# Attention output transposed by DMA from the second stage on, in a planned kernel of sparse attention and a gated FFN

## The chip, the cores and the metric

The kernel runs on one core of a Trainium2 chip. The metric is device time in microseconds, the median of several executions. Engines are named as in the profile: PE (TensorE; PEld is its weight load), DVE (VectorE), ACT (ScalarE), POOL (GpSimd), SP (SyncE, which issues the DMAs of the kernel before).

## What is computed

Attention over 4 batches, 8 heads, 768 positions and 64 dims, in which each query sees only the six chunks of 32 keys with the highest upper bounds; then a gated FFN over the 3072 tokens (512 to 1536 to 512).

```python
ub = sum(maximum(q * k_min, q * k_max), axis=-1)      # per chunk of 32 keys, causal chunks only
top_chunks = argsort(ub)[..., -6:]
scores = where(sel & causal, scale * q @ k.T, -1e9)
attn = softmax(scores)
x = (attn @ v) as [3072, 512]
out = (sigmoid(x @ w_gate) * (x @ w_val)) @ w_out
```

## The kernel before

**Stages.** The work is cut into eight stages s: batch s // 2, half s % 2 of its 384 query rows. A stage has four parts. *Load*: k, q and v come from HBM by SP's DMAs (L330 to L353). *Prep* (L379 to L539): q is transposed on PE (qT, L428) and copied by ACT or DVE into Qcat (L439 to L443); DVE forms the minimum and maximum of k by chunk (tree, L406); PE multiplies them (the bound products ub, L504), DVE takes the six best, and PE transposes the selection (apT, L533); k is cast and transposed (kT, L485). *Attention* (L550 to L625): for each head, PE writes scores into a PSUM tile (sc, L574; in odd stages two tiles per head), ACT takes the exponential (L578), POOL masks the diagonal (L584), and PE multiplies with V (pv, L596). Every two heads DVE divides by the row sums (the norm, L606 and L608) and writes the result to `xnat`, [128 rows, 3 blocks, 512] in fp16. *FFN* (L628 to L679): for each of 12 blocks PE forms gate and value products from `xT`, the transposed attention output (L646), ACT a tanh (gate, L652), DVE their product (hglu, L654); then PE forms three output tiles (o, L663), which ACT or DVE copies (osb, L670, L672) and SP stores (L678).

**The transposed attention output.** The FFN needs `xT`, two tiles per stage of [128, 2, 384]. After every four heads (L612 to L625), six PE transposes of 128x128 go into one PSUM tile of pool `m` (xtp, L621), and DVE or ACT copies it into `xT` (L624).

**The weights.** w_gate, w_val and w_out are loaded in twelve pieces of 768 KB (L367, L369) and cast by POOL or ACT (L373).

**What sets the order.** Nothing is scheduled at run time. Each step is a task with a due time, a duration per engine on which it can run, what it reads and writes, and its tiles (`Plan.add`, L70). `Plan.order` (L92) plays the tasks through: an engine takes, of those that can start within 0.12 us of the first, the one with the earliest due time. A tile of a pool can be taken only when the tile that used its buffer has been released. The result is one fixed order of instructions on each engine, with semaphore waits between them. Due times are offset by the table `NUDGE` (L22), by kind of task and by part and stage. PSUM pools are `big` (2 buffers), `m` (3) and `p` (1).

**Zero products.** When PE would idle in the planned time, the plan puts in products of zeros (`fill`, L266, and L153 to L157) that write a PSUM tile of their own in pool `p`, as long as no task has taken a tile of `p`. The first task of `p` is a kT of stage 1.

Of the kernel before, what the change touches and what calls it, by code (L numbers as in the profile page):

```python
# [9 lines left out]
F16 = mybir.dt.float16  # L10
# [4 lines left out]
GUARD = 88.0  # L15


LATENCY = {"PE": 0.22, "ACT": 0.08, "DVE": 0.06, "POOL": 0.12, "SP": 3.0}

NUDGE = {  # L22
    "v": -63.6, "Ap": -59.1, "kch": -0.4, "qch": 1.0, "wst": 2.5, "w": -706.6, "vn": -2.4, "k160": -402.8,
    "prep:0": -235.2, "tr0": 174.3, "qT0": -58.5, "Qc0": 634.5, "hq0": 22.2, "kmm0": -340.1, "kmT0": -375.7,
    "kc0": -22.3, "kT0": -50.7, "hk0": 28.9, "ub0": -139.5, "ubs0": -377.3, "ubq0": 660.7, "mx80": -334.1,
    "Ap0": -606.7, "apT0": -328.7, "mq0": -24.9, "sc0": 448.0, "attn:0": -226.6, "at0": -197.0, "pv0": 158.8,
    "xn0": 67.3, "xtp0": -203.0, "xT0": 61.1, "gv0": 102.6, "ffn:0": -24.2, "gate0": 2.6, "hglu0": -419.8,
    "o0": 643.0, "osb0": 108.2, "out0": 110.6, "k16": 506.3, "prep:1": -123.8, "tr": 10.9, "qT": -3.8, "Qc": 9.8,
    "hq": 30.7, "kmm": 15.3, "kmT": -75.4, "kc": -333.7, "kT": 3.0, "hk": 405.3, "ub": -252.3, "ubs": 344.4,
    "ubq": 8.6, "mx8": -27.8, "apT": -21.5, "mq": -5.9, "sc": -2.4, "attn:1": -132.3, "at": -49.8, "pv": -8.1,  # L30
    "xn": -608.2, "xtp": -111.2, "xT": -347.1, "gv": -3.0, "ffn:1": -26.5, "gate": -349.5, "hglu": -801.6, "o": 13.1,
    "osb": 197.5, "out": 206.7, "load:2": -53.5, "prep:2": -24.9, "attn:2": -15.6, "ffn:2": -5.1, "load:3": -28.9,
    "prep:3": -36.5, "attn:3": -33.1, "ffn:3": 8.2, "load:4": 32.8, "prep:4": -46.9, "attn:4": 31.7, "ffn:4": 18.4,
    "load:5": 20.2, "prep:5": 0.5, "attn:5": -135.7, "ffn:5": 19.7, "load:6": 25.4, "prep:6": 17.0, "attn:6": 15.6,
    "ffn:6": 217.4, "load:7": -0.8, "prep:7": 63.5, "attn:7": -95.3, "ffn:7": 359.4,
}
PARTS = {"load": ("kch", "qch", "vn", "v"), "attn": ("sc", "at", "pv", "xn", "xtp", "xT"),
         "ffn": ("gv", "gate", "hglu", "o", "osb", "out")}


# [9 lines left out]
class Plan:  # L50
# [8 lines left out]
    def __init__(self, slots, banks, cold_until=0.0, filler=None):  # L59
        self.slots = slots  # L60
        self.filler = filler
        self.banks = banks
        self.tasks = []
        self.writers, self.readers = {}, {}
        self.tile_tasks = {}
        self.cold_until = cold_until
        self.stage = None
        self.kinds = []

    def add(self, prio, options, r=(), w=(), tiles=(), port=False):  # L70
        i = len(self.tasks)

        key = w[0] if w else "-"
        kind = "const" if isinstance(key, str) else key[1] if key[0] in self.banks or key[1] == "gv" else key[0]
        names = nudged(kind, self.stage)
        self.kinds.append(names)
        prio += sum(NUDGE.get(x, 0.0) for x in names)
        deps = set()
        for key in r:
            deps.update(self.writers.get(key, ()))  # L80
            self.readers.setdefault(key, []).append(i)
        for key in w:
            deps.update(self.writers.get(key, ()))
            deps.update(self.readers.get(key, ()))
            self.writers[key] = [i]
            self.readers[key] = []
        deps.discard(i)
        for t in tiles:
            self.tile_tasks.setdefault(t, []).append(i)
        self.tasks.append((prio, options, deps, tuple(tiles), port))  # L90

    def order(self):  # L92
        n = len(self.tasks)
# [6 lines left out]
        free = {}  # L100
# [23 lines left out]
        while cand:  # L124
# [25 lines left out]
            us = self.tasks[i][1][o][1]  # L150
            if eng == "PE" and t < self.cold_until:
                us *= 2
            if eng == "PE" and self.filler and not rings[self.filler[0]]:  # L153
                each = self.filler[1] * (2 if t < self.cold_until else 1)
                fills = int((t - max(free.get("PE", 0.0), 1.0) - 0.15) / each)
                if fills > 0:
                    out.append((t - fills * each - 0.1, len(out), None, fills))  # L157
            end[i], eng_of[i] = t + us, eng
            free[eng] = t + us
            if eng == "POOL" or (eng == "DVE" and self.tasks[i][4]):  # L160
# [23 lines left out]
def kernel(  # L184
# [22 lines left out]
    R2 = CH // 2  # L207
    NST = 2 * B
    FC = D_FF // 4

    SB = {"ld": 3, "wld": 2, "vld": 2, "k16": 1, "tree": 1, "Qcat": 1, "headQ": 2, "kmx": 2, "kmm": 2, "ubs": 2,
          "mx8": 2, "rz": 2, "at": 6, "xT": 6, "xnat": 2, "gate": 3, "osb": 3, "hglu": 18}
# [17 lines left out]
    wv16 = consts.tile([128, 4, D_FF], F16, tag="wv16")  # L230
    wo16 = consts.tile([128, NFB, 512], F16, tag="wo16")

    plan = Plan({**SB, **PS}, PS, cold_until=7.0, filler=("p", 0.22, None))
    add = plan.add

    def dve_or_act(fn, dve, act):
# [26 lines left out]
        h0 = max(h0, 1) if i == 0 else h0  # L263
        copy(hks[half][i][64:89, h0:h1, :], first.to_broadcast([25, h1 - h0, HS]))

    def fill(n):  # L266

        ps = tl(("p", "fill"), [128, 512])
        for _ in range(n):
            nc.tensor.matmul(ps, zeros[:, 0:128], zeros, start=True, stop=True)  # L270

    def const_tasks():
        def _warm():
# [105 lines left out]
    def prep_tasks(s, t0, t1):  # L379
# [40 lines left out]
        for j in range(R2 // QR):  # L420
            qT = ("big", "qT", s, j) if alone else ("p", "qT", s, j)
            x = 0.05 + 0.1 * j

            def _t(j=j, qT=qT):
                ps = tl(qT, [128, QR, 128])
                for r in range(QR):
                    rr = QR * j + r
                    nc.tensor.transpose(ps[:, r, 0:RC], tl(("ld", "q", s))[0:RC, 128 * rr:128 * rr + 128], ident32[0:RC, 0:RC])  # L428
            add(at(x), [("PE", 0.40, _t)], r=[("qch", s, j), "id32"], w=[("qT", s, j)], tiles=[qT, ("ld", "q", s)])
            rs = slice(QR * j, QR * j + QR)  # L430
            for e in range(2):
                def src(j=j, e=e, qT=qT):
                    return tl(qT)[64 * e:64 * e + 64, :, 0:RC].rearrange("p r (c h) -> p h c r", h=H)

                def _raw(eng, sg, e=e, rs=rs, src=src):
                    dq = tl(("Qcat", s), [128, H, HS]).rearrange("p h (c r e) -> p h c r e", r=R2, e=2)
                    dst = dq[64 * sg:64 * sg + 64, :, :, rs, e]
                    if eng == "ACT":
                        nc.scalar.activation(dst, src(), AF.Relu if sg else AF.Copy)  # L439
                    elif sg:  # L440
                        nc.vector.tensor_scalar(dst, src(), 0.0, None, ALU.max)  # L441
                    else:
                        nc.vector.tensor_copy(dst, src())  # L443

                for sg in range(2):
                    add(at(x + 0.02), [("ACT", 0.49, lambda sg=sg, f=_raw: f("ACT", sg)),
                                       ("DVE", 0.56, lambda sg=sg, f=_raw: f("DVE", sg))][:1 if alone and j < 2 else 2],
                        r=[("qT", s, j)], w=[("Qc", s, j, e, sg)], tiles=[qT, ("Qcat", s)])
# [48 lines left out]
        for u in range(2):  # L497
# [5 lines left out]
                    h = 4 * u + i  # L503
                    nc.tensor.matmul(ps[32 * i:32 * i + 32, :], kcat[:, h, :], tl(("Qcat", s))[:, h, :], start=True, stop=True)  # L504
            x = 0.45 + 0.1 * u
            add(at(x), [("PE", 0.80, _ub)], r=qc_keys + [kkey], w=[ub], tiles=[ub, ("Qcat", s)])
            add(at(x + 0.02), [("DVE", 0.55, lambda ub=ub, ubs=ubs: nc.vector.tensor_tensor(
                tl(ubs, [128, HS]), tl(ub), penT[:, half, :], ALU.add))], r=[ub, "pen", 1, 2, 3], w=[ubs], tiles=[ub, ubs])

            def _ubq(ubs=ubs, ubq=ubq):  # L510
                ps = tl(ubq, [128, HB, 4, 32])
                for qb in range(HB):
                    nc.tensor.transpose(ps[:, qb].rearrange("p h c -> p (h c)"), tl(ubs)[:, 128 * qb:128 * qb + 128], ident32)
            add(at(x + 0.04), [("PE", 0.36, _ubq)], r=[ubs, "id32"], w=[ubq], tiles=[ubs, ubq])

            def _mx(ubq=ubq, mx8=mx8):
                m8, ps = tl(mx8, [128, HB, 4, 8]), tl(ubq)
# [32 lines left out]
    def attn_tasks(s, t0, t1):  # L550
# [12 lines left out]
        for h in range(H):  # L563
            x = h / (H + 0.5)
            for t, segs in enumerate(TILES[half]):
# [3 lines left out]
                def _sc(h=h, segs=segs, sc=sc):  # L569
# [4 lines left out]
                        nc.tensor.matmul(ps[:, 128 * o:128 * (o + n)], hk[:, h, jl:jl + 128],  # L574
                                         tl(("headQ", s))[:, h, 128 * (ib - q0):128 * (ib - q0 + n)], start=True, stop=True)
                add(at(x + 0.03 * t), [("PE", w / 2400 + 0.012 * len(segs), _sc)],
                    r=[hq_keys[h], ("mq", s, h)] + hk_keys + hkc, w=[sc], tiles=[sc, ("headQ", s)])
                add(at(x + 0.03 * t + 0.01), [("ACT", 0.19 + w * 0.815e-3, lambda sc=sc, a=a, w=w: nc.scalar.activation(  # L578
                    tl(a, [128, 1024], F16)[:, 0:w], tl(sc)[:, 0:w], AF.Exp, scale=scale))],
                    r=[sc], w=[a], tiles=[sc, a])  # L580
# [10 lines left out]
            for ib in range(q0, q0 + HB):  # L591
                def _pv(h=h, ib=ib, pv=pv):
# [3 lines left out]
                        nc.tensor.matmul(pvp[:, ib - q0, h % 2, :], tl(("at", s, h, t))[:, 128 * o:128 * o + 128],  # L596
                                         head_v(b, jb // HB)[:, h, jb % HB, :], start=(jb == 0), stop=(jb == ib))
                add(at(x + 0.9 / H + 0.01 * (ib - q0)), [("PE", 0.035 * (ib + 1), _pv)], r=ats + v_keys,
                    w=[("pv", s, h, ib)], tiles=[pv] + ats)
            if h % 2 == 1:  # L600
                hp = h // 2
                xn, rz = ("xnat", s), ("rz", s, hp)
# [1 line left out]
                def _norm(hp=hp, pv=pv, xn=xn, rz=rz):  # L604
# [4 lines left out]
                add(at(x + 0.95 / H + 0.03), [("DVE", 0.78, _norm)],  # L609
                    r=[("pv", s, hh, ib) for hh in (h - 1, h) for ib in range(q0, q0 + HB)], w=[("xn", s, hp)],  # L610
                    tiles=[pv, xn, rz])
            if h % 4 == 3:  # L612
                u = h // 4
                xtp, xT = ("m", "xtp", s, u), ("xT", s, u)

# [12 lines left out]
    def ffn_tasks(s, t0, t1):  # L628
# [4 lines left out]
        for fb in range(NFB):  # L633
# [7 lines left out]
            for i in range(2):  # L641
# [6 lines left out]
                for c0 in (0, 2):  # L648
                    add(at(x + 0.025 * i + 0.005 * c0), [("PE", 0.34, lambda c0=c0, f=_mm: f(c0))],
                        r=[("xT", s, 0), ("xT", s, 1), ("w", 2 * (fb // 3) + i)], w=[(s, "gv", i, fb)],  # L650
                        tiles=[gv[i], ("xT", s, c0 // 2)])
            add(at(x) - EV, [("ACT", 0.49, lambda gate=gate, ps=ps: nc.scalar.activation(  # L652
                tl(gate, [128, HS], F16), ps(0), AF.Tanh, scale=0.5))], r=[(s, "gv", 0, fb)], w=[gate], tiles=[gv[0], gate])
            add(at(x) - EV, [("DVE", 0.55, lambda gate=gate, hg=hg, ps=ps: nc.vector.scalar_tensor_tensor(  # L654
# [47 lines left out]
        ffn_tasks(s, T[s + 1] - (12 if s == 0 else 0) + 4, T[s + 1] + W + 4)  # L702
    with tc.manual_schedule():
        for i, o in plan.order():
            if i is None:
                fill(o)
            else:
                plan.tasks[i][1][o][2]()


# [28 lines left out]
```

## Time and profile before

| what | us |
|---|---|
| median of 3 runs (lowest, highest) | 340.85 (338.41, 341.76) |
| profiled execution, its own time | 340.61 |
| its span, first to last instruction | 338.9 |
| PE busy | 319.9 |
| DVE busy | 242.0 |
| ACT busy | 223.0 |
| POOL busy | 107.0 |

Busy times are unions: matmuls overlap, so the sum of durations is larger than the busy time, and what one instruction takes from PE is read from the distance of starts. A group's line gives line, engine, operation, output<-inputs, sizes and count, then busy us, mean ns of one, then the idle time of the engine just before and what ended it. In a timeline the columns are start, duration, engine, line, operation and count. "Granted clock" is the share of full speed that TensorE was given.

### The profile page before, as it was taken

To read this page: it belongs to the slowest core of one execution; us is meant where nothing else is said; L and a number is where in the kernel's file an instruction comes from. 1 tells how busy PE (TensorE), PEld (TensorE's weight loads), DVE (VectorE), ACT (ScalarE), POOL (GpSimd) and SP (SyncE) were. 2 spreads that over 40 slices of the span, in tenths; PEclk is the share of its full clock that TensorE was granted. 3 is DMA by queue.
4 is the path that set the end of the run, shared out by engine and by line. 5 is a ranking of instruction groups with operands and counts; after the bars stand their busy time and mean duration, and the time that the engine had idled before them with its cause. 6 is when DMAs were issued, how large, how long until landed. Compare 5 with 4: busy or idle time off the path is not lost.

```text
span 338.9 us, 7406 instructions
## 1 busy us (share of the span) xinstructions
PE 319.9 (94%) x2855; PEld 193.5 (57%) x2855; DVE 242.0 (71%) x642; ACT 223.0 (66%) x336; POOL 107.0 (32%) x147
## 2 busy tenths in 40 slices
PE   8886889979999989999999999999999999999995
PEld 3445445756457536675556556766666546775552
DVE  5779678869999899997986699886656257532430
ACT  5798964968467635886567669985856235993331
POOL 8278574553423330225110612240310030210000
PEclk9999699999999999999999999999999999999999
DMA  5997999977983150304630313000000010001002
GB/s 147 238 296 219 249 258 312 265 172 143 215 194 95 32 154 4 95 0 116 155 94 14 93 64 119 10 0 3 33 31 33 31 65 2 2 2 72 23 0 93
DMA packets 37947, 35.08 MB, mean 103 GB/s; under 512 B 25944, under 2 KB 30040, under 8 KB 36952
## 3 DMA queue, kind: packets, MB, share of 16 engines
q1 hardware_dynamic: 37912, 34.61, 37.6%
q8 instruction: 22, 0.36, 0.5%
q14 instruction: 13, 0.11, 0.1%
HBM read 28.31 MB, written 6.29 MB: 102 GB/s over the span
## 4 chain that ended last, share of the span: by engine, by line
PE 67%; DVE 14%; ACT 6%; POOL 5%; DMA 4%; issue 3%; DVEq 0%; ACTq 0%
PE m_o L663 15%; PE m_g L646 12%; PE m_v L646 11%; PE big_sc L574 7%; PE m_pv L596 5%; PE big_gv L646 5%; DMA wld<-in_moe_w_out_dram 4%; ACT Qcat L439 3%; PE p_qT L428 3%; DVE tree L406 3%; PE p_ub L504 3%; PE p_fill L270 3%; DVE hglu L654 2%; DVE Qcat L441 2%; DVE Qcat L443 2%
## 5 line engine op out<-in xcount | busy, mean ns | idle before, releaser
L578 ACT ACTIVATE at<-big_sc 128x896 f16<-128x896 f32 (+1 forms) x96 | 83.9, 916 | 12.3 <-PE big_sc L574 9.9
L646 PE MATMUL m_v<-xT,wv 128*128 128x384 f16 x336 | 72.7, 330 | 0.9 <-DVE hglu L654 0.9
L646 PE MATMUL m_g<-xT,wg 128*128 128x384 f16 x336 | 73.0, 330 | 0.5 <-DVE hglu L654 0.3
L663 PE MATMUL m_o<-wo,hglu 128*128 128x512 f16 x288 | 72.0, 379 | 0.0
L584 POOL TENSOR_SCALAR_AFFINE_SELECT at<-at 128x384 f16<-128x384 f16 x64 | 35.8, 562 | 108.2 <-ACT at L578 100.4
L652 ACT ACTIVATE gate<-m_g 128x384 f16<-128x384 f32 x84 | 41.0, 490 | 32.9 <-PE m_g L646 27.4
L654 DVE SCALAR_TENSOR_TENSOR hglu<-gate,m_v 128x384 f16<-128x384 f16 x84 | 46.0, 550 | 14.3 <-PE m_v L646 9.2
L646 PEld LDWEIGHTS <-wg 128*128 128x128 f16 x384 | 36.4, 99 | 24.9 <-issue 4.9
L646 PEld LDWEIGHTS <-wv 128*128 128x128 f16 x384 | 36.4, 99 | 24.6 <-issue 4.7
L574 PE MATMUL big_sc<-headQ,headK 89*128 89x128 f16 (+2 forms) x480 | 48.5, 240 | 0.7 <-DVE headQ L537 0.2
L663 PEld LDWEIGHTS <-hglu 128*128 128x128 f16 x288 | 26.2, 98 | 23.7 <-issue 1.9
L574 PEld LDWEIGHTS <-headK 89*128 89x128 f16 x480 | 32.2, 97 | 9.8 <-issue 2.0
L596 PEld LDWEIGHTS <-at 128*128 128x128 f16 x672 | 27.3, 98 | 15.3 <-ACT at L578 6.1
L455 POOL CAST headQ<-Qcat 64x768 f16<-64x768 f32 x31 | 26.1, 873 | 30.6 <-DVE Qcat L443 28.8
L596 PE MATMUL m_pv<-v,at 128*128 128x65 f16 x672 | 31.8, 194 | 3.8 <-POOL at L584 3.7
L670 ACT ACTIVATE osb<-m_o 128x512 f32<-128x512 f32 x20 | 11.9, 597 | 31.9 <-PE m_o L663 31.7
L406 DVE TENSOR_TENSOR tree<-tree 96x512 f32<-96x512 f32 (+2 forms) x48 | 28.9, 603 | 1.1
L393 POOL CAST k<-ld_k 96x1024 f16<-96x1024 f32 x12 | 14.1, 1190 | 47.8 <-PE p_kT L485 37.8
L443 DVE COPY Qcat<-p_qT 64x384 f32<-64x384 f32 x35 | 19.4, 555 | 13.5 <-PE p_qT L428 12.0
L439 ACT ACTIVATE Qcat<-p_qT 64x384 f32<-64x384 f32 x45 | 22.2, 493 | 6.8 <-PE p_qT L428 2.9
L406 DVE TENSOR_TENSOR tree<-ld_k 96x1024 f32<-96x1024 f32 (+1 forms) x18 | 20.6, 1149 | 2.1 <-DMA ld_k<-in_k_dram 2.0
L441 DVE TENSOR_SCALAR Qcat<-p_qT 64x384 f32<-64x384 f32 x32 | 17.8, 557 | 1.8 <-ACT Qcat L439 1.2
(91 smaller groups left out, 364.1 us busy)
## 6 DMA issues: line engine op xcount, KB each, us to landing
vld<-in_v_dram SPq DMA_DIRECT2D x24, 256.0 KB
out_dram<-osb SPq DMA_DIRECT2D x24, 256.0 KB
ld_k<-in_k_dram SPq DMA_DIRECT2D x5, 768.0 KB
ld_q<-in_q_dram SPq DMA_DIRECT2D x5, 768.0 KB
wld<-in_moe_w_gate_dram SPq DMA_DIRECT2D x4, 768.0 KB
wld<-in_moe_w_val_dram SPq DMA_DIRECT2D x4, 768.0 KB
wld<-in_moe_w_out_dram SPq DMA_DIRECT2D x4, 768.0 KB
ld_k<-in_k_dram SPq DMA_DIRECT2D x12, 192.0 KB
```

The lines of the kernel that those rows point to most:

```text
L406: nc.vector.tensor_tensor(dst[:, a:e], src[0:RC, a:e], src[0:RC, n + a:n + e], op)
L439: nc.scalar.activation(dst, src(), AF.Relu if sg else AF.Copy)
L443: nc.vector.tensor_copy(dst, src())
L455: eng.tensor_copy(tl(("headQ", s), [89, H, HS], F16)[0:64, h:h + 2, :], tl(("Qcat", s))[0:64, h:h + 2, :])
L574: nc.tensor.matmul(ps[:, 128 * o:128 * (o + n)], hk[:, h, jl:jl + 128], tl(("headQ", s))[:, h, 128 * (ib - q0):128 * (ib - q0 + n)], start ...
L578: add(at(x + 0.03 * t + 0.01), [("ACT", 0.19 + w * 0.815e-3, lambda sc=sc, a=a, w=w: nc.scalar.activation(tl(a, [128, 1024], F16)[:, 0:w], ...
L584: nc.gpsimd.affine_select(out=dg, in_=dg, compare_op=ALU.is_ge, fill=0.0, base=0, pattern=[[0, HB], [1, 128]], channel_multiplier=-1)
L596: nc.tensor.matmul(pvp[:, ib - q0, h % 2, :], tl(("at", s, h, t))[:, 128 * o:128 * o + 128], head_v(b, jb // HB)[:, h, jb % HB, :], start= ...
L646: nc.tensor.matmul(ps(i), w16[:, c, 128 * fb:128 * fb + 128], tl(("xT", s, c // 2))[:, c % 2, :], start=(c == 0), stop=(c == 3))
L652: add(at(x) - EV, [("ACT", 0.49, lambda gate=gate, ps=ps: nc.scalar.activation(tl(gate, [128, HS], F16), ps(0), AF.Tanh, scale=0.5))], r=[ ...
L654: add(at(x) - EV, [("DVE", 0.55, lambda gate=gate, hg=hg, ps=ps: nc.vector.scalar_tensor_tensor(tl(hg, [128, HS], F16), tl(gate), 1.0, ps( ...
L663: nc.tensor.matmul(tl(o, [128, 512]), tl(("hglu", s, fc))[:, 128 * tb:128 * tb + 128], wo16[:, fc, :], start=(fc == 0), stop=(fc == NFB - 1))
```

## The change

1. From stage 1 on, the six PE transposes and the copy are replaced by three DMAs that transpose, issued on ACT's queue, one for each block of 128 rows: `xnat` [128, 256] to `xT` [128, 2, 128]. In the plan they take ACT 0.2 us and land 2.2 us later. Stage 0 keeps PE. This makes 42 DMAs in 14 groups. Since each DMA semaphore serves every eighth DMA, an issue also waits for the DMA eight places before it in the program.
2. Zero products no longer have a tile of their own. They are written into the tile of the PE task that follows them, if that task is the first to use the tile, and after the buffer is free; they are planned up to 60 us instead of until `p` is first used. There are 43 (63 before): 29 and 1 before the first two qT groups, 5 before the first bound products, 2 before the first scores, 4 before the last products with V and 2 before the first gate product of stage 0.
3. All due-time offsets (`NUDGE`) are new, so the order of tasks changes on every engine. In stage 0 DVE, ACT and POOL keep their order but for a few neighbours; later the parts of the stages interleave differently. On SP the last two weight pieces are now issued after the q parts of stage 2.

```diff
-LATENCY = {"PE": 0.22, "ACT": 0.08, "DVE": 0.06, "POOL": 0.12, "SP": 3.0}
+LATENCY = {"PE": 0.22, "ACT": 0.08, "DVE": 0.06, "POOL": 0.12, "SP": 3.0, "XQ": 0.1}
 NUDGE = {
-    "v": -63.6, "Ap": -59.1, "kch": -0.4, "qch": 1.0, "wst": 2.5, "w": -706.6, "vn": -2.4, "k160": -402.8,
+    "v": -37.2, "Ap": 21.5, "kch": -2.8, "qch": -2.2, "wst": -2.8, "w": -573.6, "vn": -6.3, "k160": -367.7,
...
-            if eng == "PE" and self.filler and not rings[self.filler[0]]:
-                each = self.filler[1] * (2 if t < self.cold_until else 1)
-                fills = int((t - max(free.get("PE", 0.0), 1.0) - 0.15) / each)
-                if fills > 0:
-                    out.append((t - fills * each - 0.1, len(out), None, fills))
+            if eng == "PE" and t < self.filler[1] and i in self.fill_tile:
+                each = self.filler[0] * (2 if t < self.cold_until else 1)
+                fills = int((t - max(free.get("PE", 0.0), slot_time(i), 1.0) - 0.25) / each)
+                if fills > 0 and self.tasks[i][3][0] not in given:
+                    self.fills[i] = fills
...
-    plan = Plan({**SB, **PS}, PS, cold_until=7.0, filler=("p", 0.22, None))
+    plan = Plan({**SB, **PS}, PS, cold_until=7.0, filler=(0.22, 60.0))
...
-    def fill(n):
-        ps = tl(("p", "fill"), [128, 512])
+    def fill(ps, n):
         for _ in range(n):
-            nc.tensor.matmul(ps, zeros[:, 0:128], zeros, start=True, stop=True)
+            nc.tensor.matmul(ps, zeros[:, 0:128], zeros[:, 0:ps.shape[-1]], start=True, stop=True)
...
-            if h % 4 == 3:
+            if h % 4 == 3 and s >= XQ:
+                u = h // 4
+                xT, xk = ("xT", s, u), ("xq", s, u)
+
+                def _xq(u=u, xT=xT):
+                    for ib in range(HB):
+                        nc.scalar.dma_start_transpose(tl(xT, [128, 2, HS], F16)[:, :, 128 * ib:128 * ib + 128],
+                                                      tl(("xnat", s))[:, ib, 256 * u:256 * u + 256])
+                add(at(x + 1.1 / H + 0.02), [("ACT", 0.2, _xq)], r=[("xn", s, 2 * u), ("xn", s, 2 * u + 1)], w=[xk],
+                    tiles=[xT, ("xnat", s)])
+                add(at(x + 1.1 / H + 0.02), [("XQ", 2.2, None)], r=[xk], w=[xT], tiles=[xT, ("xnat", s)])
+            elif h % 4 == 3:
                 u = h // 4
                 xtp, xT = ("m", "xtp", s, u), ("xT", s, u)
```

The tasks qT, ub, ubq, sc, pv and the gate and value products get an argument `fill=` that names their tile; XQ is 1.

## Prediction

> **What bounds the kernel now.** I read the page first (busy times, slices), then busy time in stretches of 10 us, then groups by line, then the timeline of TensorE (PE) and of the load queue around the places that the change touches.
>
> The page:
> ```profile
> span 338.9 us, 7406 instructions
> PE 319.9 (94%) x2855; PEld 193.5 (57%) x2855; DVE 242.0 (71%) x642; ACT 223.0 (66%) x336; POOL 107.0 (32%) x147
> ```
> PE is busy 94% of the span; no other engine comes near. By stretches (start:end, length, then busy us and count for PE, PEld, DVE, ACT, POOL, then clock, DMA share, GB/s):
> ```profile
> 30.00:40.00 10.00, 6.54 (x66) 4.29 (x65) 7.47 (x15) 8.31 (x14) 8.48 (x10) 0.79 0.78 198
> 80.00:90.00 10.00, 9.95 (x80) 4.62 (x78) 9.67 (x19) 7.27 (x12) 6.24 (x6) 1.00 0.68 161
> 90.00:100.00 10.00, 10.00 (x74) 6.15 (x71) 9.04 (x29) 5.22 (x11) 0.22 (x1) 1.00 1.04 237
> 200.00:210.00 10.00, 9.73 (x100) 6.57 (x98) 9.50 (x32) 9.47 (x15) 2.82 (x3) 1.00 0.27 92
> 290.00:300.00 10.00, 10.00 (x148) 7.44 (x146) 5.01 (x14) 9.70 (x15) 2.08 (x4) 1.00 0.01 2
> ```
> From 50 us on PE sets the pace; while the odd stages' exps run (200 to 210, 290 to 300), ACT is nearly as full. The clock is below 1 from 30 to 40 (0.79; still 0.87 from 40 to 50). The groups that go, and the timeline of one of them on PE:
> ```profile
> L621 PE MATMUL m_xtp<-ident,xnat 128*128 128x128 f16 x96 | 8.3, 222 | 0.7 <-DVE xnat L608 0.7
> L624 ACT COPY xT<-m_xtp 128x768 f16<-128x768 f16 x7 | 5.6, 798 | 1.5 <-PE m_xtp L621 1.4
> L624 DVE COPY xT<-m_xtp 128x768 f16<-128x768 f16 x9 | 5.0, 556 | 2.1 <-PE m_xtp L621 2.0
> ```
> ```profile
> 84.33 0.50 PE L621 MATMUL m_xtp<-ident,xnat 128*128 128x128 f16 x6
> 84.66 1.03 PE L663 MATMUL m_o<-wo,hglu 128*128 128x512 f16 x4
> ```
> Six transposes show 0.50 us, but the next product starts 0.33 us after the first of them: that is what one group takes from PE. DMA issues, seen on SP's queue:
> ```profile
> 33.14 0.37 SPq L367 DMA_DIRECT2D wld<-in_moe_w_gate_dram  x1
> 33.55 0.51 SPq L335 DMA_DIRECT2D vld<-in_v_dram  x1
> ...
> 85.94 7.41 SPq L335 DMA_DIRECT2D vld<-in_v_dram  x3
> ...
> 136.96 0.81 SPq L331 DMA_DIRECT2D ld_q<-in_q_dram  x1
> ```
> An issue holds its queue for 0.37 to 0.81 us, and longer when the DMA engines are full (2.5 us each at 86).
>
> **The sum's base.** The profiled execution took 340.61 us, span 338.9 plus 1.7 around it, 0.24 below the median of 340.85. I add to 340.6.
>
> **PE's transposes.** Stages 1 to 7 lose two groups each: 14 x 0.34 = -4.8 us, all on PE, which hardly idles there. It counts in full unless something else makes PE wait, since PE's order is fixed. The 14 evictions (0.56 on DVE or 0.80 on ACT) also go; neither engine ends the work, so I count 0 for them. Stage 0 keeps its two groups.
>
> **The DMA transposes at the start of an FFN.** The first gate product of a stage needs both halves of xT. Before: norm, transposes, copy. After: norm on DVE (192 + 558 ns, with hand-overs 1.05 us), three issues on ACT, landing. No row shows a DMA transpose. Issue: bounds 0.34 (a store) and 0.81 (the 96x2048 load); I take 0.43, nearest to the small rows since a piece is only 64 KB, so X = 1.3 us for three. Landing: at the end SP waited 1.5 us for the last store; the first 192 KB parts reached DVE about 2.9 us after their issue; I take 2.2. Together 4.55 us (bounds 3.6 and 6.4). The cover is what stands in PE's order between the last product with V and the first gate product, at 0.216 per output product and 0.78 per bound product: 3.4 us in stage 1, 4.9 in 2, 4.8 in 3, 15 in 4, 9.7 in 5, 17 in 6, 4.75 in 7. So only stage 1 waits, 1.2 us, and there the DMA engines are full (share 0.68 to 1.04 at 80 to 100), for which I add 1.0: +2.2. Upper bound, with X = 2.4 and a landing of 7.4 in stage 1, 2.9 elsewhere: 7.5 + 1.5 + 1.6 + 1.6 = 12.2; lower 0.2.
>
> A rule that speaks against the change is in the Trainium skill, "VectorE: DVE Perf Modes", The three transpose paths: a 128x128 transpose takes 390 ns on TensorE and 1309 ns through the DMA crossbar, so TensorE is preferred where PSUM will do. PE's row has six in 0.50 us, far below that page; no row shows the crossbar. Six crossbar transposes one after another would be 7.9 us, an estimate from that page; the four short covers would then be overrun by some 18 us, and the sum would be near 354.
>
> **ACT's queue.** ACT gets 42 issues, 18 us at 0.43, for the 5.6 us of copies. Behind them stand exps and Qcat copies, for which PE waits in turn. In stages 1, 3, 5 and 7 the first half's issues stand between exps, where ACT is up to 97% busy. There one exp (0.92 us) runs while ACT issues; what exceeds it, 4 x (1.3 - 0.92) = +1.5, I charge to PE. Bounds: 0 and 4 x 2.4 = 9.7. Elsewhere ACT is under 75% busy: 0. Each issue also waits for the DMA eight places earlier, SP's loads and stores among them; by the order of the program those are long issued, 0. SP's stores wait likewise for transposes; SP idles for over 150 us in such waits, 0.
>
> **Zero products and the clock.** Before, 63 of them (16.8 us busy), 33 standing between the prep steps from 9.9 to 24 us. After, 43, but only six between the first qT group and the bound products, because the other tiles aren't free: from 10.7 to 19.0 PE gets three prep groups and five short fills, some 2.0 us of work in 8.3. What that does, the 1 us stretches of PE show (busy, clock, DMA share, GB/s):
> ```profile
> 32.00:33.00 1.00, 0.51 (x12) 1.00 0.00 0
> 33.00:34.00 1.00, 0.36 (x6) 1.00 0.00 0
> 34.00:35.00 1.00, 0.19 (x2) 1.00 0.88 74
> 35.00:36.00 1.00, 0.71 (x13) 0.88 0.83 295
> 36.00:37.00 1.00, 0.57 (x4) 0.50 1.06 398
> ...
> 42.00:43.00 1.00, 1.00 (x6) 0.70 0.07 20
> ```
> About 45% busy over four us was followed by half clock for 6.8 us. So I expect the dip at some 14 to 16 us: the bound products (1.43 us), their transposes (0.77) and a first score tile at half clock put 2.2 us on the start of stage 0's attention. The six fills before the last products with V and the first gate product, and PE's backlog, then keep the clock up at 36 to 43, which gives back 3.0 (6.8 us at half clock did at most 3.4 us of work, with some waits among them). Bounds: -3.0 (only the second) and +4.5 (half clock until 43); I take +0.5, since part of a delay is absorbed at 69.7, where PE waits 1.75 us for POOL's weight casts. "TensorE: Matmul & The Clock Gate", Why this matters for your kernels, asks only for no idle gaps above about 3 us; here the clock fell with no gap above 1.13 us. By that page the new gaps (up to 1.7 us) would cost nothing.
>
> **New due times.** Attention of stages 4 and 6 moves ahead of the older FFN (covers 2.0 to 15, 14.6 to 17 us); POOL now masks head 3 of stage 1 before the last weight cast; SP issues the last two weight loads after the q parts. Gains and losses up to the 1.75 us of that wait; I take 0.
>
> Sum: 340.6 - 4.8 + 2.2 + 1.5 + 0.5 = 340.0.
>
> **Rivals.** (a) All hidden: landing and issues inside the covers, the clock kept: 340.6 - 4.8 + 0.2 (the lower bound of the waits), and up to 3.0 less by the clock: 333 to 336, middle 335. For it: PE at 94%, ACT's idle third. Against: stage 1's cover of 3.4. (b) Slower: ACT is held by the issues, at X = 2.4 (the 0.81 row): waits 5.8, exps 5.9, clock 0.5, so 348. It decides from X = 1.95, 0.65 us per issue, on. For it: each transpose writes two runs of 256 bytes in each of 128 partitions, where the simplest issues above write one, and ACT's 97%. Against: the 0.34 and 0.37 rows. (c) The fills don't do what they are for: half clock until 43, +4.5 for +0.5: 344.
>
> **How the numbers follow.** Forecast 0.33 (337.4 to 344.3 its own range, a tenth of it beyond), (a) 0.32, (b) 0.28, (c) 0.07, half of it slower. Measurement tells about 1% from no change, 3.4 us. Faster 0.32, same 0.33, slower 0.35. Range: from all of (a) at 333 to 355, between (b) at 348 and all upper bounds together (362).
>
> **What would show it.** PE's busy time after 50 us down by 4.8; no m_xtp after stage 0. PE's wait before m_g of stage 1 for DMA about 2 us, near none in stages 4 to 6. ACT's issue rows 0.3 to 0.6 us: above 0.65 means (b). Clock 0.5 between 14 and 26 us and 1.0 at 36 to 43. Wrong if issues hold ACT far longer than any row here, or if the clock stays up early.

## The result, and the profile after

The changed kernel takes 381.11 us (median of 4 runs, 376.84 to 382.55), against 340.12 for the kernel before, run beside it: a ratio of 1.116 between the fast runs, 95% interval 1.105 to 1.128. It is 41 us slower; 340.0 was forecast, with a range that ended at 355.

The page of the changed kernel, its busy times, its clock by slices and its chain of work:
```profile
span 378.9 us, 7255 instructions
PE 326.3 (86%) x2751; PEld 192.3 (51%) x2751; DVE 233.7 (62%) x625; ACT 217.4 (57%) x338; POOL 104.0 (27%) x148
...
PEclk9789899968599999999899999989998899989999
...
PE 59%; DVE 10%; ACT 10%; ACTq 8%; DMA 5%; issue 5%; POOL 1%; DVEq 0%; SPq 0%
```
Before, the clock's line and the chain were:
```profile
PEclk9999699999999999999999999999999999999999
...
PE 67%; DVE 14%; ACT 6%; POOL 5%; DMA 4%; issue 3%; DVEq 0%; ACTq 0%
```
PE executes 104 products fewer and is busy 6.4 us longer. The rest of the growth is idle time of PE: 378.9 - 326.3 = 52.6 us, where it was 338.9 - 319.9 = 19.0. Every other engine is less busy than before, so no engine has taken over as the bound by its work. What is new on the chain is "ACTq", ACT's queue, with 8%; and the clock, which was at 9 in all slices but the fifth, now falls in several places.

The same stretches of 10 us as before the change (columns as there):
```profile
30.00:40.00 10.00, 7.08 (x87) 4.99 (x87) 8.81 (x16) 9.26 (x14) 9.73 (x12) 1.00 0.65 157
80.00:90.00 10.00, 9.06 (x85) 5.80 (x84) 5.21 (x10) 5.24 (x9) 3.52 (x4) 0.71 0.92 178
90.00:100.00 10.00, 4.83 (x20) 1.23 (x24) 3.20 (x4) 1.58 (x3) 2.25 (x3) 0.63 1.17 216
200.00:210.00 10.00, 6.88 (x73) 4.73 (x71) 3.69 (x9) 5.81 (x12) 2.08 (x4) 1.00 0.15 30
290.00:300.00 10.00, 7.22 (x33) 3.87 (x33) 2.90 (x6) 2.83 (x6) 0.00 (x0) 0.66 0.07 13
```
The front has lost nothing to speak of (30 to 40). From 80 us on, PE falls from nearly 10 to between 4.8 and 9.1, and DVE and ACT fall with it, POOL in three of these four stretches: they wait too. (The same stretch doesn't hold the same work in both kernels.)

What they wait for stands in the row of the new issues, with the shortest, median and longest duration in ns and the first and last start:
```profile
L636 ACTq DMA_TRANSPOSE xT<-xnat x42: 1182/1264/2273, 74.5 to 349.5; - x42
```
An issue holds ACT's queue for 1.26 us, not 0.43: three of them for 3.8 us, 42 for 53 us. ACT's timeline at the first group, in stage 1 (start, us, engine, line, operation; in brackets the idle time before and what ended it):
```profile
74.46 1.28 ACTq L636 DMA_TRANSPOSE xT<-xnat  x1
74.47 0.91 ACT L596 ACTIVATE at<-big_sc 128x896 f16<-128x896 f32 x1
75.78 3.08 ACTq L636 DMA_TRANSPOSE xT<-xnat  x2
78.96 1.02 ACT L596 ACTIVATE at<-big_sc 128x1024 f16<-128x1024 f32 x1 [3.57 <-issue]
```
One exp, sent off before the issues, runs beside them. The next one has its scores ready and starts 3.57 us after the end of the last. On PE, at the same place:
```profile
76.71 0.60 PE L692 MATMUL m_o<-wo,hglu 128*128 128x512 f16 x2
80.03 1.01 PE L591 MATMUL big_sc<-headQ,headK 89*128 89x384 f16 x4 [2.73 <-ACT at L596]
```
PE goes on for 2.85 us with what was ready, and then waits for a score buffer that the held exp has to empty. Stretches of 1 us show what follows (start:end, length, PE, PEld, DVE, ACT, POOL, clock, DMA share, GB/s):
```profile
78.00:79.00 1.00, 0.00 (x0) 0.00 (x0) 0.96 (x3) 0.04 (x1) 0.00 (x0) 1.00 0.20 25
79.00:80.00 1.00, 0.00 (x0) 0.00 (x0) 0.90 (x4) 1.00 (x2) 0.00 (x0) 0.50 0.84 252
...
84.00:85.00 1.00, 1.00 (x10) 0.67 (x8) 0.75 (x3) 0.43 (x1) 0.16 (x1) 0.50 1.37 181
85.00:86.00 1.00, 1.00 (x5) 0.42 (x3) 1.00 (x1) 0.00 (x0) 0.00 (x0) 0.59 1.19 209
```
At 79.0, 1.7 us into this wait of 2.7, the clock falls to half and stays there for 6.8 us, until 85.8; a pair of output products that took 0.60 us at 76.71 takes 1.06 at 80.84. That is why PE is busy longer with fewer products. So a group can be paid twice, as a wait and in the clock.

In the waits, these delays are easily misread (engine and line, what it waited for: us in total, times, longest):
```profile
ACT Qcat L454 <- DMA xT<-xnat: 13.8, 4, 4.1
ACT osb L699 <- DMA xT<-xnat: 8.9, 2, 5.4
```
Neither of these activations reads xT. The wait is put down to the DMA before it in the queue, of which only the issuing was waited for; the run e4_dma_nobody_reads, below, shows that.

### The profile page after: what moved, and what is told of

The parts are those of the page before. It is cut to its first block, busy times and chain, and to the rows that moved or that the text cites. A ratio compares the mean times of both kernels' runs of the same rounds, so it can differ in the third digit from the quotient of the medians.

```text
span 378.9 us, 7255 instructions
## 1 busy us (share of the span) xinstructions
PE 326.3 (86%) x2751; PEld 192.3 (51%) x2751; DVE 233.7 (62%) x625; ACT 217.4 (57%) x338; POOL 104.0 (27%) x148
## 4 chain that ended last, share of the span: by engine, by line
PE 59%; DVE 10%; ACT 10%; ACTq 8%; DMA 5%; issue 5%; POOL 1%; DVEq 0%; SPq 0%
PE m_v L675 12%; PE m_o L692 11%; PE m_g L675 11%; ACTq L636 8%; PE big_sc L591 6%; PE m_pv L614 4%; PE big_gv L675 4%; DMA xT<-xnat 3%; ACT at L596 3%; PE p_ub L519 3%; ACT Qcat L454 3%; PE big_qT L276 2%; DVE tree L420 2%; DVE xnat L626 2%; DMA ld_q<-in_q_dram 2%
## 5 line engine op out<-in xcount | busy, mean ns | idle before, releaser
L675 PE MATMUL m_v<-xT,wv 128*128 128x384 f16 x336 | 75.0, 338 | 10.4 <-ACT gate L681 10.4
L675 PE MATMUL m_g<-xT,wg 128*128 128x384 f16 x336 | 77.0, 342 | 3.1 <-DMA xT<-xnat 2.9
L602 POOL TENSOR_SCALAR_AFFINE_SELECT at<-at 128x384 f16<-128x384 f16 x64 | 34.1, 535 | 97.4 <-ACT at L596 96.9
L591 PE MATMUL big_sc<-headQ,headK 89*128 89x128 f16 (+2 forms) x480 | 50.1, 245 | 3.5 <-ACT at L596 3.2
L454 ACT ACTIVATE Qcat<-p_qT 64x384 f32<-64x384 f32 x64 | 31.3, 490 | 25.6 <-DMA xT<-xnat 13.8
L470 POOL CAST headQ<-Qcat 64x768 f16<-64x768 f32 x30 | 25.0, 866 | 63.4 <-DVE Qcat L458 32.1
L614 PE MATMUL m_pv<-v,at 128*128 128x65 f16 x672 | 32.9, 198 | 4.1 <-ACT at L596 4.1
L614 PEld LDWEIGHTS <-at 128*128 128x128 f16 x672 | 28.8, 101 | 14.9 <-ACT at L596 8.8
L456 DVE TENSOR_SCALAR Qcat<-p_qT 64x384 f32<-64x384 f32 x24 | 13.4, 557 | 19.5 <-ACT Qcat L454 19.2
L442 PE MATMUL p_qT<-ident,ld_q 96*128 96x96 f32 x112 | 15.3, 261 | 6.8 <-ACT Qcat L454 5.6
```

What stands on the lines that cost most here:

```text
L470: eng.tensor_copy(tl(("headQ", s), [89, H, HS], F16)[0:64, h:h + 2, :], tl(("Qcat", s))[0:64, h:h + 2, :])
L602: nc.gpsimd.affine_select(out=dg, in_=dg, compare_op=ALU.is_ge, fill=0.0, base=0, pattern=[[0, HB], [1, 128]], channel_multiplier=-1)
L675: nc.tensor.matmul(ps(i), w16[:, c, 128 * fb:128 * fb + 128], tl(("xT", s, c // 2))[:, c % 2, :], start=(c == 0), stop=(c == 3))
```

## The experiments

The theories put to the test: H, the issues hold ACT's queue; L, the landing of the transposes holds up the FFN; O, the new order and the new zero products are what costs. The kernel before, run beside each set, had medians of 339.49 us (e1 to e4), 339.48 (e5, e6, e7, e10) and 341.52 (e8, e11, e12); runs of different sets are compared by their ratios to it.

### e1_no_transposes and e4_dma_nobody_reads: the hold by itself

e1 keeps the order of the changed kernel on every engine and issues no transposes; the FFN of stages 1 to 7 reads stage 0's xT. e4 issues all 42, and the FFN still reads stage 0's xT, so that nobody waits for a landing.
```diff
e1 (and, without its second pair of lines, e4):
-tl(("xT", s, c // 2))[:, c % 2, :]
+tl(("xT", 0, c // 2))[:, c % 2, :]
-[("ACT", 0.2, _xq)]
+[("ACT", 0.2, None)]
```


> The changed kernel in its own order on every engine, but without the 42 transposing DMAs: from stage 1 on the FFN reads the xT tiles of stage 0, so the attention output of stages 1 to 7 isn't used and nothing waits for it. Theory H (each issue holds ACT's queue, 1.26 us in the trace after, 3.8 a group, 53 us in all, and PE idles behind ACT): 333 to 339, since order and zero products cost little. Theory L (the landing before the FFN's first gate product is the loss): the same 333 to 339. Theory O (the new order and the moved zero products are the loss): above 350.

> As the run without transposes, with the 42 transposing DMAs back on ACT's queue in their places, but nobody waits for what they write (the FFN still reads stage 0's xT, so the output is not that of the reference). H: 360 to 380, most of the changed kernel's 381. L: 333 to 345, as without them. O: as without them.

Measured: e1 335.54 us, ratio 0.987 (0.984 to 0.991); e4 377.19, ratio 1.110 (1.104 to 1.115). The 42 issues, waited for by no one, cost 41.7 us; what waits for the landing adds less than 1% (1.116 against 1.110, the intervals overlap). H holds, O falls: the new order and zero products, with neither PE's transposes nor the DMAs, are 1.3% faster than before. The pages split the cost, since both have the same products in the same order. The busy times of e1:
```profile
PE 312.1 (94%) x2751; PEld 187.8 (56%) x2751; DVE 233.5 (70%) x625; ACT 218.0 (65%) x338; POOL 104.4 (31%) x148
```
and those of e4:
```profile
PE 326.8 (87%) x2751; PEld 193.5 (52%) x2751; DVE 233.7 (62%) x625; ACT 217.5 (58%) x338; POOL 104.3 (28%) x148
```
The spans are 333.8 and 375.2. PE's idle time grows from 21.7 to 48.4 us (+26.7), and the same 2751 products take 14.7 us longer, at a mean clock of 0.936 in place of 0.978. That the DMAs' traffic does it, and not their issue, is still open here; e3 settles it.

### e3_issue_on_sp: the same DMAs from another queue

```diff
-nc.scalar.dma_start_transpose(
+nc.sync.dma_start_transpose(
```


> The changed kernel with the 42 issues on SP's queue instead of ACT's; the order of PE, ACT, DVE and POOL is the same, the whole result is computed. SP idles for over 200 us. H: 340 to 352, ACT is free again, what is left are landings and issues of 3.8 us a group before the FFNs of stages 1, 2, 3 and 7 (covers 3.4 to 4.9). L: 365 to 381. O: above 370.

Measured: 341.18 us, ratio 1.005 (1.001 to 1.008). One word takes back 38 us by the ratios (1.116 to 1.005), with the same traffic. The issues are as long on SP:
```profile
L636 SPq DMA_TRANSPOSE xT<-xnat x42: 1168/1237/2526, 72.1 to 309.3; - x42
```
SP has the time: its waits for the output copies alone come to 45.6 us, and few wait for what stands behind. Left over against e1 are 1.7%, 5.6 us, about as much as PE now waits for the landing (4.3 us before products in m_g, in stages 1, 2 and 3, and 0.9 in the last stage).

### e12_second_half_on_act: which groups cost

e3 with the second group of each stage back on ACT, where the forecast counted nothing. (It counted nothing for the first groups of stages 2, 4 and 6 either.)
```diff
-nc.sync.dma_start_transpose(
+(nc.scalar if u else nc.sync).dma_start_transpose(
```


> e3_issue_on_sp with the second group of every stage (21 of 42 issues) back on ACT's queue and the first group left on SP. The forecast charged the first groups alone (between exps, ACT up to 97% busy) and gave the second groups 0, since ACT is under 75% busy there: by that step the time stays at 341 to 343. Theory H': a held queue costs at either place, since the next activation behind it is one that PE waits for soon: half of the 40 us between 341 and 381, so 355 to 368.

Measured: 367.14 us, ratio 1.078 (1.071 to 1.085). The second groups cost 7.4% (25 us) over e3, the first groups the remaining 3.8% (13 us). ACT at the second group of stage 1:
```profile
83.63 4.92 ACTq L636 DMA_TRANSPOSE xT<-xnat  x3
88.60 0.49 ACT L454 ACTIVATE Qcat<-p_qT 64x384 f32<-64x384 f32 x1 [5.15 <-issue]
```
and on PE behind it:
```profile
89.14 1.00 PE L519 MATMUL p_ub<-Qcat,kcat 128*32 128x384 f32 x8 [4.21 <-ACT Qcat L454]
```
Behind the issues of the other second groups stand output copies, tanhs of the gate and a kT copy; PE waits up to 1.5, 5.0 and 3.1 us for these, though ACT as a whole has time (busy 60% of the span).

### e10_plain_copies: is it the transposing?

The changed kernel with plain copies from ACT's queue in place of the transposing ones; the FFN of stages 1 to 7 reads data that isn't transposed.
```diff
-nc.scalar.dma_start_transpose(xT piece, xnat piece)
+nc.scalar.dma_start(xT piece, xnat piece.rearrange("p (a c) -> p a c", a=2))
```


> The changed kernel with 42 plain copies of 128x256 in place of the 42 transposing ones, on ACT's queue at the same places, so that the FFN of stages 1 to 7 reads what isn't transposed (the transposing is left out). T, the hold belongs to the transposing issue: a plain issue holds ACT for 0.3 to 0.8 us, as SP's rows do, and the time is 340 to 360 (13 to 34 us held in place of 53). D, any DMA issue from ACT's queue holds it as long: 1.2 us each, 375 to 382.

Measured: 353.68 us, ratio 1.041 (1.034 to 1.048).
```profile
L636 ACTq DMA_DIRECT2D xT<-xnat x42: 601/632/1811, 73.4 to 319.6; - x42
```
A plain issue of the same piece holds the queue for 0.63 us, half as long: T holds. And at 26.5 us held, the kernel is still 5.4% (18 us) slower than e1; 5.1 us of that are a wait for the landing in stage 1. So the forecast's price of 0.43 us for each, 18 us held, would probably not have been nearly free either; no run has that price.

### e5_six_pieces and e6_whole_rows: what an issue's price goes by

Both issue on SP and keep e3's order. e5 moves each piece in two of 128x128; e6 moves three of 128x512 a stage, at the place of the second group.
```diff
e5:
+for i in range(2):
+    c0 = 256 * u + 128 * i
+    nc.sync.dma_start_transpose(xT[:, i, 128 * ib:128 * ib + 128], xnat[:, ib, c0:c0 + 128])
e6:
+if u == 1:
+    for ib in range(HB):
+        nc.sync.dma_start_transpose(xw[:, :, 128 * ib:128 * ib + 128], xnat[:, ib, :])
```


> e3_issue_on_sp with each transfer of 128x256 cut into two of 128x128: 84 issues on SP in place of 42, the same bytes, the same order elsewhere. F, the hold of the queue is a fixed price for an issue: each still holds SP for about 1.2 us, six hold it for 7.4 us a group, and the kernel gets slower than e3 (341) by 5 to 15 us. Z, the hold goes with the size: each holds SP for about 0.65 us, and the time stays within 2 us of 341.

> e3_issue_on_sp with three transfers of 128x512 a stage at the place of the second group, in place of six of 128x256: 21 issues on SP, the same bytes, the same order of PE, ACT, DVE and POOL. F, a fixed price for an issue: 1.2 us each, SP held for 26 us less in all, 337 to 340. Z, the hold goes with the size: 2.3 to 2.5 us each, 7 us at the end of every stage, no first group landed early, 341 to 346.

The row of the issues in e5:
```profile
L638 SPq DMA_TRANSPOSE xT<-xnat x84: 1093/1224/5682, 72.1 to 328.2; - x84
```
and in e6:
```profile
L638 SPq DMA_TRANSPOSE xw<-xnat x21: 1196/1257/1697, 84.1 to 312.2; - x21
```
1.22 us for 128x128, 1.24 for 128x256, 1.26 for 128x512: a fixed price for an issue (F). e5 took 362.09 us (a single run), 21 above e3 and more than F's 5 to 15: PE waits 16.0 us before m_g for the last of six, 3.5 in the last stage, and is busy 7 us longer (mean clock 0.948, in e3 0.969). e6 took 343.97, ratio 1.012 (1.006 to 1.017), above F's 337 to 340 and inside Z's 341 to 346, though Z's price is wrong. F is right on the price and was wrong on its worth: SP had time to spare, so fewer issues freed nothing, and the first products of an FFN, which in e3 run on the early first group, now wait for the last issue too (6.3 us before m_g in place of 4.3).

### e2_before_with_dma and e7_fills_alone: the other two parts

e2 is the kernel before, its due times and zero products kept, with the transposing DMAs on ACT. e7 is the kernel before with the new kind of zero products alone (XQ = 8 and the old NUDGE).

> The kernel before with its own due times and its 63 zero products, and only the transposes of stages 1 to 7 moved to DMAs on ACT's queue. H: 365 to 390, since the hold is the same and this order is not made for it. L: 365 to 390 too. O: 336 to 345.

> The kernel before, its transposes and due times, with the changed kernel's zero products (into the tile of the product that follows, until 60 us) in place of its own (into a free tile). PE's instructions change in the zero products alone; the other engines keep their order. Theory O' (the gain of 1.3% that the order without transposes showed over before comes from the zero products too): 336 to 339. Rival: the zero products are worth nothing, or cost, since both kinds stop and the half clock comes anyway: 339 to 343.

Measured: e2 407.16 us, ratio 1.197 (1.192 to 1.202), above the 390 that H allowed; e7 341.13, ratio 1.003 (1.000 to 1.007). With the issues on ACT, the old due times (with the old zero products) are 7% (26 us) worse than the new ones, so it also matters where in the order the issues stand. In the old order the zero products alone cost about 0.35%, 1.2 us, hardly told from nothing; O' is wrong, and the gain in e1 isn't theirs.

### e8_both_fills and e11_sp_planned: a version that is faster

e8 is e3 with both kinds of zero products: the 63 into a tile of their own, and of the new kind those 6 that come after them (4 before the last products with V, 2 before the first gate product), 69 and not 63 + 43. e11 also tells the planner what an issue takes, and has new due times for it.
```diff
-add(at(x + 1.1 / H + 0.02), [("ACT", 0.2, _xq)], ...
-add(at(x + 1.1 / H + 0.02), [("XQ", 2.2, None)], ...
+add(at(x + 1.1 / H + 0.02), [("SP", 4.0, _xq)], ...
+add(at(x + 1.1 / H + 0.02), [("XQ", -1.5, None)], ...
```
(The planner adds 3.0 us to whatever leaves SP, so that -1.5 makes a landing of 1.5.)

> e3_issue_on_sp (transfers issued on SP, 341) with the 63 zero products of the kernel before, into a free tile, beside its own 43; the order of everything else is that of e3. Theory C: part of what e3 loses to the order without transposes (335.5) is half clock in the first 40 us, where its clock was 0.81 in the mean; with both kinds of fill the clock stays up as in the kernel before, and the time is 337 to 339.5. Rival: more fills change nothing or stand in the way, 340.5 to 344.

> The transfers issued on SP, both kinds of zero products, and a new order: the planner is told 4.0 us of SP for each group of three issues, with the landing 1.5 us after their end, where it had been told 0.2 us of ACT and 2.2 us, and new due times are searched for with these prices. If what was wrong with the change was the price and the queue alone, the new order gets near the time without transposes: 335 to 338.5, 0.5 to 1.2% below the kernel before. Rival: the landing and the half clock at the start, which the planner doesn't see, eat it up: 339.5 to 343.

Measured: e8 340.12 us, ratio 0.995 (0.991 to 0.999); e11 338.39, ratio 0.992 (0.988 to 0.996). Each has to be held against 341.52 for the kernel before in this set: by the ratio e8 is about 1% better than e3, as C has it, though its median lies above C's range. Its clock is higher as well: the means of its ten runs are 0.979 to 0.998, those of e3 0.965 to 0.985. e11 beats both kernels, by 0.8% and 11%. Its page:
```profile
span 336.9 us, 7314 instructions
...
PE 316.0 (94%) x2777; PEld 187.9 (56%) x2777; DVE 234.0 (69%) x625; ACT 216.6 (64%) x335; POOL 110.9 (33%) x151
```
PE is 3.9 us less busy than in the kernel before and idle for 20.9 us, 1.9 more; no wait for the transposes is among its longest. It stays 0.4 points above e1, and the intervals overlap. Those of e8 and e11 overlap too, so what the measured price and the new due times add to e8 isn't shown, nor which of the two does it.

## Why the prediction was wrong, step by step

**PE's transposes, -4.8: not contradicted, but not measured alone.** e1, with neither PE's transposes nor the DMAs, is 1.3% faster than before, 4.3 us; the forecast's terms for it, -4.8 + 0.5 + 0, give 4.3 too. But e1 also has the new order and zero products, and if these cost more than 0.5, as below, the agreement is partly luck. PE's busy time after 50 us falls from 278.7 to 276.0 in e1, not by 4.8, but the cut at 50 us doesn't divide the two orders at the same work. In the changed kernel itself it rises to 290.1, so the sign that was named failed there for another reason, the half clock.

**Wait at the start of the FFN, +2.2: the place right, the parts wrong.** PE waits 2.9 us before m_g in stage 1 and in none of stages 2 to 6 (0.9 in stage 7), nearly as forecast. That is luck: in e3, where nothing holds ACT, PE waits in all four stages with short covers (2.7 us in stage 1, 0.7 to 0.9 in 2, 3 and 7); in the changed kernel it is, it seems, already delayed enough by the holds. And in stage 1 the issues last 3.9 us, not 1.3, and the landing is 6.3 us (last issue done at 91.7, product at 98.0, with the DMA engines full). With free engines, in e3, it is 1.1 to 1.3 us, not 2.2.

**ACT's queue, +1.5: the step that failed.** "Issue: bounds 0.34 (a store) and 0.81 (the 96x2048 load); I take 0.43" is the mis-sized term: 1.26 measured, above its upper bound. Both bounds came from plain issues; no row showed a transposing one. The forecast's own sign of being wrong, "issues hold ACT far longer than any row here", is what the trace shows. "Elsewhere ACT is under 75% busy: 0" failed as well, and costs more: with the true price, the forecast's own formulas give 4 x (3.8 - 0.92) = 11.5 for the odd stages and, with a norm of 1.05 and a landing of 1.2, 6.4 for the four short covers. The sum would have been 354, 27 below what was measured. What is missing is about the second groups, 25 us by e12. A mean share says how often ACT has work, not how soon PE needs the next piece of it: at the first group above PE had work left for 2.85 us, while the hold lasts 4.4 and the exp behind it ends 5.5 us after the hold began; the difference is the wait of 2.7. The formulas also have no term for the clock: of e4's 41 us over e1, 15 are products that take longer at the lower clock.

**Rival (b)** named the mechanism, the place and the sign ("ACT's issue rows 0.3 to 0.6 us: above 0.65 means (b)"), and priced it at 348 by the 0.81 row. It was right in kind; only its price was far too small. Its argument for it, that a transposing issue writes more runs, isn't what decides: the plain copy of the same piece takes 0.63 us.

The Trainium skill, "VectorE: DVE Perf Modes", The three transpose paths, had been weighed against the change, with a sum near 354. Its 1309 ns is near an issue's 1.22 us for one 128x128 block. But a 128x512 piece, four blocks, is issued in 1.26 us, so the figure isn't a price for each block here. It had the sign right and was nearer than 340, but by another path: it put some 18 us on waits before the FFNs, where the trace has 2.9 and 0.9.

**Zero products, +0.5: the right sign, the size open.** e7 gives +1.2 for them in the old order. In the new order e8, with the old kind put back, is 1.0% faster than e3, some 3.3 us; by that the term is too small. In the changed kernel the clock fell at 14, as said, but came back at 21 and not at 26. Its stretches of 1 us, the clock third from the end:
```profile
14.00:15.00 1.00, 0.00 (x0) 0.00 (x0) 0.45 (x3) 0.98 (x3) 0.00 (x0) 0.57 1.29 215
...
21.00:22.00 1.00, 1.00 (x15) 0.23 (x8) 0.56 (x1) 0.82 (x1) 1.00 (x2) 1.00 0.80 240
```
It stayed up at 36 to 43, as forecast, and fell again at 44.9:
```profile
42.00:43.00 1.00, 0.47 (x3) 0.09 (x1) 1.00 (x1) 1.00 (x2) 0.00 (x0) 1.00 0.67 132
...
45.00:46.00 1.00, 1.00 (x6) 0.78 (x6) 0.93 (x3) 0.92 (x3) 0.29 (x1) 0.50 0.96 361
```
Rival (c), half clock until 43, did not come about. That the six late zero products are what kept the clock up isn't shown: e3 has the same ones in the same order and was at half clock from 38.1 to 41.5.

**New due times, 0: not neutral.** Without issues on ACT no run measures them alone; with them they save 7% (e2 against the changed kernel), though they were made for a plan in which a group's issues take ACT 0.2 us.

## What to carry to other kernels

Before work is moved to a DMA, ask how long its issue holds the queue of the engine that issues it, and take that from a row of the same kind of DMA; a row of a plain one is no bound for a transposing one. If an engine also hands buffers back to the bound engine, a hold there can cost whatever it and the work behind it exceed the bound engine's backlog (here 5.5 us against 2.85), however low the engine's busy share, and again in the clock; issue from a queue on which nobody waits. A planner that is told a wrong price lays the work out for it; the fastest kernel here that computes the whole result was planned with the measured one, though its lead over e8 isn't clear of the noise.

## What the runs showed of the hardware

- A transposing DMA from SBUF to SBUF holds the queue that issues it for a median of 1.22 to 1.26 us (shortest 1.09), on ACT and on SP alike for 128x256, and on SP for 128x128 and 128x512; a plain one of 128x256 for 0.60 to 0.63. The Trainium skill, "DMA: Bandwidth & Descriptors", Issuing engines are not separate DMA queues, says that issuing from several engines only saves the time it takes to initiate a DMA, "which is usually small relative to the DMA itself". Here it isn't small: 1.26 us against a landing of 1.1 to 1.3 us, and where it was spent decided 38 us.
- An activation sent off before the issue runs beside it (0.91 us at 74.47, beside an issue of 1.28 at 74.46); one that stands behind the issues waits (3.57 us, until 78.96).
- In the changed kernel half clock came 1.7 us into a wait of PE of 2.7 us (77.3 to 80.0) and lasted 6.8 us; it came at the end of a wait of 2.3 us (42.5 to 44.8) and lasted 3.4. The Trainium skill, "TensorE: Matmul & The Clock Gate", Why this matters for your kernels, warns of idle gaps above about 3 us; here shorter ones were enough. In e3 the clock fell at 38.1 with no wait of PE above 0.72 us in the four us before, so the length of one gap doesn't decide it.
